# Block-sparse attention and a folded FFN: all engine orders from a list schedule, crossbar transposes, a shorter mask chain, value units of one head pair

## Chip, cores, metric

One core of one Trainium2 chip. The time is device microseconds of one execution; lower is better. Kernels of one set of rounds ran on the same chip with the kernel before beside them, and only runs marked fast are compared. This program runs on one core, so "slow" here only means a run over 1.5% above that kernel's fastest.

## The reference

Four batches, 8 heads, 768 positions, head size 64. Each 32x32 block of scores is kept or masked (window, first and last block row and column, three sampled blocks per row). The attention output becomes the 3072 x 512 input of an FFN without activation:

```python
scores = np.where(mask, q @ k.T / 8, -1e9)
attn   = softmax(scores) @ v                   # (B, H, S, D)
x      = attn.transpose(0, 2, 1, 3).reshape(B * S, H * D)
out    = ((x @ w1) * (x @ w2)) @ w3 @ w_out    # w3 @ w_out can be folded once
```

## The kernel before

The order on TensorE, ScalarE and VectorE is written by hand; GpSimd (POOL) issues all loads, which cast f32 to bf16 on the way. One step of the main loop does two score tiles (two head pairs), the values of the step before, and two filler pieces (of the fold w3 @ w_out, or of the FFN). q, k and x are turned on TensorE through PSUM; v gets its column of ones on GpSimd. PSUM: two score tiles of two banks, one value tile of two banks, two filler banks.

```python
def transposes(b, pr):                                  # q and k of a head pair, on TensorE
    tp = ps_s.tile([128, 2, 1024], BF16, tag="s")
    for x, src in ((0, qn[b, pr]), (1, kn[b, pr])):
        for c in range(C):
            for h in range(2):
                nc.tensor.transpose(tp[64*h:64*h+64, x, c*128:(c+1)*128], src[:, h, c, :], ident)
    nc.vector.tensor_copy(t, tp[:, :, :S])
def widen(b, pr):
    nc.gpsimd.memset(t[:, :, :, D:], 1.0)
    nc.gpsimd.tensor_copy(t[:, :, :, :D], vn[b, pr])    # behind the loads in POOL's queue
def scores(b, t, Q, kp, i):
    ...                                                 # 4 matmuls of 64 rows, 256 columns
    nc.scalar.activation(e, s, AF.Exp, scale=1.0 / 8.0)
    nc.vector.tensor_tensor(e, e, mask[...], op=ALU.mult)
...
for s, g in enumerate(groups):
    scores(b, t, Q, kp, 0)
    scores(b, t, Q, kp, 1)          # two score tiles in one visit to the 64-row mode
    values(*prev); turned(); finish(prev)
    ...
    pop(0 if s < 3 else 2)          # filler
```

The softmax here doesn't subtract the row's maximum and nothing guards it: scores larger than these inputs give would overflow.

## Time and profile before

| | before |
|---|---|
| time, median | 321.65 us |
| TensorE busy / VectorE / ScalarE | 261.4 / 207.5 / 171.2 us |

The top of the page of before: busy time by engine, then tenths of busy time in 40 slices of 8 us (PE is TensorE).

```profile
PE 261.4 (81%) x2932; PEld 141.6 (44%) x2932; DVE 207.5 (65%) x355; ACT 171.2 (53%) x202; POOL 61.1 (19%) x105
PE   0570388878889889998899889999988999889994
DMA  7999995956433000273301100001000010002003
```

In the views s is a score tile, e its exponentials, o the value accumulator, xn the normalised attention output and x the same turned; a, pb and h are FFN tiles; qkt is q and k turned, and in the change qs is q or k re-packed for the crossbar and f a filler bank.

TensorE has a thin start and small holes afterwards; the DMA engines are full for about 55 us and then mostly free. TensorE's timeline between 22 and 38 us (start, length, line, operation, tiles, shape, count, and in brackets the idle time before it and what ended it):

```profile
23.16 0.61 PE L206 MATMUL s<-qkt 64*128 64x256 bf16 x4 [0.30 <-ACT e L211]
36.73 0.38 PE L230 MATMUL o<-v,e 128*128 128x65 bf16 x4 [12.96 <-POOL v L195]
```

One hole of 13 us: v is there, but its widening stands behind the weight loads in POOL's queue. TensorE's waits over the whole run (total us, times, longest):

```profile
PE o L230 <- POOL v L195: 13.4, 2, 13.0
PE o L230 <- DVE xn L248: 11.1, 16, 1.9
PE pb L310 <- ACT a L302: 7.6, 11, 0.7
```

A stretch of the steady part, from the timeline:

```profile
165.67 1.03 PE L310 MATMUL pb<-x,w_sb 128*128 128x512 bf16 x4
166.63 0.61 PE L206 MATMUL s<-qkt 64*128 64x256 bf16 x8
167.17 0.66 PE L230 MATMUL o<-v,e 128*128 128x65 bf16 x16
```

From start to start, 8 score matmuls (two tiles) take 167.17 - 166.63 = 0.54 us, changes of the array's mode included (score matmuls use 64 rows of the array, the others 128; a visit to the 64-row mode is an unbroken run of score matmuls). Lengths overlap the next group and are not used for costs.

### The profile page before, as it was taken

To read this page: it belongs to the slowest core of one execution; us is meant where nothing else is said; L and a number is where in the kernel's file an instruction comes from. 1 tells how busy PE (TensorE), PEld (TensorE's weight loads), DVE (VectorE), ACT (ScalarE), POOL (GpSimd) and SP (SyncE) were. 2 spreads that over 40 slices of the span, in tenths; PEclk is the share of its full clock that TensorE was granted. 3 is DMA by queue.
4 is the path that set the end of the run, shared out by engine and by line. 5 is a ranking of instruction groups with operands and counts; after the bars stand their busy time and mean duration, and the time that the engine had idled before them with its cause. 6 is when DMAs were issued, how large, how long until landed. Compare 5 with 4: busy or idle time off the path is not lost.

```text
span 320.9 us, 6905 instructions
## 1 busy us (share of the span) xinstructions
PE 261.4 (81%) x2932; PEld 141.6 (44%) x2932; DVE 207.5 (65%) x355; ACT 171.2 (53%) x202; POOL 61.1 (19%) x105
## 2 busy tenths in 40 slices
PE   0570388878889889998899889999988999889994
PEld 0330255555544445555444445555444454444441
DVE  3611089888886677778767676787676876743432
ACT  1091166654566667465865686647666666620220
POOL 8535666813250000115300000000000000000000
PEclk9999999999999999999999999999999999999999
DMA  7999995956433000273301100001000010002003
GB/s 106 141 204 207 209 204 81 162 87 87 65 49 51 0 2 18 86 129 52 51 1 67 65 2 2 2 33 67 35 1 2 34 67 35 0 2 112 19 2 131
DMA packets 19922, 21.41 MB, mean 67 GB/s; under 512 B 1460, under 2 KB 14772, under 8 KB 19892
## 3 DMA queue, kind: packets, MB, share of 16 engines
q0 software_dynamic: 16400, 14.68, 30.2%
q1 hardware_dynamic: 3492, 6.29, 5.2%
q8 instruction: 23, 0.38, 0.5%
q14 instruction: 7, 0.06, 0.1%
HBM read 29.36 MB, written 6.29 MB: 111 GB/s over the span
## 4 chain that ended last, share of the span: by engine, by line
PE 54%; DVE 14%; ACT 11%; issue 8%; DMA 7%; POOL 4%; ACTq 0%; POOLq 0%
PE pb L310 11%; PE pa L299 11%; ACT e L211 9%; PE po L320 9%; PE o L230 8%; DMA w_sb<-in_moe_w_dram 7%; DVE e L212 7%; PE s L206 7%; DVE xn L248 4%; PE wp L281 4%; PE tp L186 2%; ACT a L302 2%; DVE qkt L189 2%; PE xp L254 2%; DVE rec L246 1%
## 5 line engine op out<-in xcount | busy, mean ns | idle before, releaser
L211 ACT ACTIVATE e<-s 128x1024 bf16<-128x1024 f32 x144 | 139.3, 1022 | 87.1 <-PE s L206 86.6
L212 DVE TENSOR_TENSOR e<-e,mask 128x1024 bf16<-128x1024 bf16 x144 | 104.1, 729 | 60.9 <-ACT e L211 59.2
L230 PE MATMUL o<-v,e 128*128 128x65 bf16 x1152 | 49.6, 196 | 25.3 <-POOL v L195 13.4
L230 PEld LDWEIGHTS <-e 128*128 128x128 bf16 x1152 | 40.3, 99 | 42.7 <-issue 25.3
L310 PE MATMUL pb<-x,w_sb 128*128 128x512 bf16 x192 | 49.2, 378 | 7.6 <-ACT a L302 7.6
L206 PE MATMUL s<-qkt 64*128 64x256 bf16 x576 | 48.0, 278 | 6.1 <-ACT e L211 3.6
L312 DVE TENSOR_TENSOR h<-pb,a 128x512 bf16<-128x512 f32 x48 | 33.1, 689 | 28.8 <-PE pb L310 28.8
L299 PE MATMUL pa<-x,w_sb 128*128 128x512 bf16 x192 | 49.3, 379 | 0.0
L302 ACT CAST a<-pa 128x512 bf16<-128x512 f32 x48 | 28.3, 589 | 36.1 <-PE pa L299 36.1
L320 PE MATMUL po<-wf_sb,h 128*128 128x512 bf16 x192 | 44.4, 379 | 0.0
L206 PEld LDWEIGHTS <-qkt 64*128 64x128 bf16 x576 | 22.9, 95 | 37.9 <-issue 34.9
L310 PEld LDWEIGHTS <-w_sb 128*128 128x128 bf16 x192 | 18.6, 97 | 33.5 <-issue 13.3
L320 PEld LDWEIGHTS <-h 128*128 128x128 bf16 x192 | 17.8, 98 | 19.2
L86 POOL DMA_DIRECT2D qn<-in_q_dram x16 | 11.7, 728 | 69.8 <-PE tp L186 61.3
L299 PEld LDWEIGHTS <-w_sb 128*128 128x128 bf16 x192 | 16.4, 98 | 14.2
L325 DVE COPY ob<-po 128x512 f32<-128x512 f32 x24 | 16.5, 686 | 9.5 <-PE po L320 9.5
L248 DVE TENSOR_TENSOR xn<-o,rec 128x512 bf16<-128x512 f32 x24 | 16.6, 691 | 0.8
L195 POOL COPY v<-vn 128x768 bf16<-128x768 bf16 x16 | 15.5, 980 | 3.1 <-DMA vn<-in_v_dram 3.0
L189 DVE COPY qkt<-tp 128x1536 bf16<-128x1536 bf16 x16 | 15.2, 948 | 1.3 <-PE tp L186 1.3
L281 PE MATMUL wp<-wo_sb,w3t_sb 128*128 128x512 bf16 x64 | 15.1, 379 | 0.0
L174 ACT CAST mask<-mp 128x512 bf16<-128x512 f32 x9 | 4.9, 587 | 14.3 <-PE mp L172 14.3
L86 POOL DMA_DIRECT2D kn<-in_k_dram x16 | 11.7, 730 | 3.4 <-PE w3p L268 1.7
(46 smaller groups left out, 129.9 us busy)
## 6 DMA issues: line engine op xcount, KB each, us to landing
out_dram<-ob SPq DMA_DIRECT2D x24, 256.0 KB, 2.0
w_sb<-in_moe_w_dram POOLq DMA_DIRECT2D x16, 256.0 KB, 10.2
qn<-in_q_dram POOLq DMA_DIRECT2D x16, 192.0 KB, 3.6
kn<-in_k_dram POOLq DMA_DIRECT2D x16, 192.0 KB, 4.4
vn<-in_v_dram POOLq DMA_DIRECT2D x16, 192.0 KB, 4.8
wo_sb<-in_moe_w_out_dram POOLq DMA_DIRECT2D x1, 1024.0 KB, 12.2
rand_sb<-in_sampled_blocks_dram SPq DMA_DIRECT2D x1, 0.6 KB
```

What stands on the lines that cost most here:

```text
L86: nc.gpsimd.dma_start(out=t, in_=src[b][:, 2 * pr:2 * pr + 2])
L206: nc.tensor.matmul(s[:, h, k2 * QT:(k2 + 1) * QT], lhsT=qk[64 * h:64 * h + 64, 1, kc * 128:(kc + 1) * 128], rhs=qk[64 * h:64 * h + 64, 0, ...
L211: nc.scalar.activation(e, s, AF.Exp, scale=1.0 / 8.0)
L212: nc.vector.tensor_tensor(e, e, mask[:, t, kp:kp + 1, :].to_broadcast((128, 2, 512)), op=ALU.mult)
L230: nc.tensor.matmul(o[:, qt, g * (D + 1):(g + 1) * (D + 1)], lhsT=es[i][:, h, lo:lo + 128], rhs=V1[b, 2 * Q + i][:, h, kc, :], start=kc == ...
L248: nc.vector.tensor_tensor(xn, o[:, :, :, :D], rec.to_broadcast((128, 2, 4, D)), op=ALU.mult)
L281: nc.tensor.matmul(box["p"], lhsT=w3t_sb[:, j, i * 128:(i + 1) * 128], rhs=wo_sb[:, j, :], start=j == 0, stop=j == NF - 1)
L299: nc.tensor.matmul(p, lhsT=w1_sb[:, c, f * 128:(f + 1) * 128], rhs=x[:, c, :], start=c == 0, stop=c == 3)
L302: nc.scalar.copy(a, p)
L310: nc.tensor.matmul(p, lhsT=w2_sb[:, c, f * 128:(f + 1) * 128], rhs=x[:, c, :], start=c == 0, stop=c == 3)
L312: nc.vector.tensor_tensor(hT[:, f, :], p, box["a"], op=ALU.mult)
L320: nc.tensor.matmul(box["o"], lhsT=hT[:, f, n * 128:(n + 1) * 128], rhs=wf_sb[:, f, :], start=f == 0, stop=f == NF - 1)
```

## The change

The intent: take work off TensorE (q, k of batches 1 to 3 and all of x are turned by DMA transposes through the crossbar), fill its holes (every engine's order, POOL's and SyncE's too, comes from a list schedule worked out at build time from fixed durations), and free PSUM (value units of one head pair need one bank, so there are three filler banks).

```diff
+class Plan:                      # list schedule over tasks: costs by engine, deps, buffers
+                for d in t.deps:
+                    e = d.seen                        # seen = end + 0.22 us for TensorE,
+                    base = max(base, e)               # for a TensorE task after another too
+            elif t.kind == "xbar":
+                xbar = max(xbar, t.end + 1.6) + t.bytes / 250e3
+                t.seen = xbar + 0.4                   # q or k, 196608 bytes: 2.8 us in all
...                               (the rest of the planner cut)
-    t = qkt.tile(...); nc.vector.tensor_copy(t, tp[:, :, :S])
+            if b == 0:            # on TensorE, as before
+            ...
+            else:                 # q, k of batches 1 to 3
+                m = add(f"re {b}{pr}{x}", {DVE: 0.45}, ... nc.vector.tensor_copy(
+                    T(*mid), T(*src).rearrange("p h c d -> p c h d")), ...)      # mid: qs, 3 buffers
+                t = add(f"xb {b}{pr}{x}", {SP: 0.3}, ... nc.sync.dma_start(
+                    out=T(*dst)[:, x, :]..., in_=T(*mid)..., transpose=True), kind="xbar", ...)
+    # x: one crossbar transpose of xn for each 128 rows
+    t = add(f"xx {b}{t3}{qt}", {SP: 0.3}, ... nc.sync.dma_start(out=T("x", i)[...],
+                    in_=T(*xk)[:, qt, :], transpose=True), kind="xbar", ...)
-        nc.gpsimd.tensor_copy(t[:, :, :, :D], vn[b, pr])
+        nc.vector.tensor_copy(w[:, :, :, :D], T(*src))
+    ts = add(f"S {sk}", {PE: 0.216}, sc, deps=QK[b, pr] + [prev_s], mode="S", ...)
+    # masks from fewer VectorE instructions; FFN pieces of two matmuls; copies on ScalarE or VectorE
```

## The prediction

> **What bounds the kernel now**
>
> - 0 to 40 us (table of stretches): TensorE is busy 13.4 of 40 us. By the chain of waits the worst hole is 13.4 us for the first widened v (POOL v L195): v was issued at 5.5 us, but its widening stands behind some 20 weight-load issues in POOL's in-order queue and starts at 35.8 us. ScalarE and VectorE idle 14 us with it.
> - 40 to 281 us: cadences read from the timeline are 0.54 us for two score tiles with mode switches, 0.48 for 16 value matmuls, 0.216 for a 512-column matmul, 0.79 for 24 q/k transposes, 0.22 for 4 x transposes. That is about 188 us of TensorE work in 241. The list of waits names the holes: values on xn (11 us), pb on a (7.6; only two filler banks), exp on scores (72.6).
> - 281 to 321 us: TensorE runs two FFN units back to back; the others are nearly idle.
>
> **What the change does**
>
> - TensorE loses 12 q/k transposes x 0.79 = 9.5 us and 24 x transposes x 0.22 = 5.3 us. Left: 72 x 0.54 + 72 x 0.48 + 640 x 0.216 + about 10 (fold transposes, batch 0, masks) = 222 us.
> - VectorE: minus 12 qkt copies x 0.95 and 24 x copies x 0.42 (21 us); plus re-packing q, k (11), v widening from POOL (10), twice as many rec/xn (5). About 210 us, of which 39 may go to ScalarE (masks, fold copies, ob). ScalarE: 144 x 0.97 + 48 x 0.58 + its share, about 190. Neither binds before TensorE.
> - DMA: 48 crossbar transposes, 7.9 MB. The Trainium skill, "DMA: Bandwidth & Descriptors", section "Latency and other measured facts", gives 261 GB/s for a DMA transpose with a non-contiguous middle dimension: an estimate of 0.8 us for 196 KB, plus about 2 us fixed; no run here shows it yet. The DMA engines are mostly under 10% busy after 100 us, so it fits.
> - Start: mask chain about 2 us shorter; v widened as it lands, values near 10 us instead of 36.7. Batch 0's 36 exps (35 us) and the fold (17 us of TensorE) run under the weight loads, which end near 45 us.
> - One-bank value accumulator, three filler banks, list schedule: waits are filled with FFN pieces of two matmuls.
>
> **Critical path.** TensorE is the limit: 222 us of work, 11 us of start in which it can't be fed, 3 us for the last copy and store: 236 us. With 8% for holes: **254 us**, 8 in 10 within **243 to 272**. Of 68 us won, about 15 are removed work, 20 the start, 33 fewer holes. Faster by over 2%: 0.96; within 2%: 0.02; slower: 0.02.
>
> **What would show each step.** TensorE over 90% from 45 us to the end; no wait of values on v; first values before 15 us; transposes of batches 1 to 3 and of x gone from TensorE, cadences unchanged; exp's idle time filled with a and ob copies; crossbar transposes landing in under 5 us; at most about 40 us of pure FFN at the end.
>
> **What would make it wrong.** Crossbar transposes several times slower than estimated, or slowed by loads on the same DMA engines: then scores wait for qkt, FFN for x. In-order engines following a schedule with wrong durations: small waits everywhere, TensorE near 80%. VectorE dearer than assumed (strided widening, more small operations) and so the limit. Loads held back because buffers free late.

## More of the kernel before

Busy time by stage (columns: stretch, its length, busy us with instructions for PE, PEld, DVE, ACT, POOL, granted clock, DMA share, GB/s):

```profile
60.00:125.00 65.00, 55.65 (x731) 31.92 (x730) 49.47 (x85) 40.76 (x46) 13.62 (x21) 1.00 0.38 53
125.00:240.00 115.00, 103.96 (x1263) 56.70 (x1261) 85.52 (x138) 73.12 (x85) 9.86 (x16) 1.00 0.18 43
```

## The result

The change took 297.79 us (296.79 and 298.79) against 321.65: ratio 0.9258, 95% interval 0.9124 to 0.9392. Timed again over more rounds (below) it took 297.36 us, ratio 0.9215 (0.9189 to 0.9241). It is faster, but far outside the predicted 243 to 272 us. The ratios are from the fast runs of both kernels in the same rounds, so they are not quite the ratios of the medians.

The same lines after the change, the top of the page (with the granted clock, PEclk, whose row was 9 in every slice before):

```profile
PE 256.7 (87%) x2505; PEld 121.0 (41%) x2548; DVE 185.4 (63%) x396; ACT 184.6 (63%) x221; POOL 46.2 (16%) x75
PE   2989999768689995699999999799999999948994
PEclk9999999997959997999999999999999999995998
DMA  6999999699989999936750101301014001130003
```

The start is full now. But TensorE has a weak stretch in slices 8 to 16 (60 to 125 us), where the DMA row stays at 8 or 9, and a hole near the end; behind each the clock row dips. TensorE's waits:

```profile
PE f L576 <- DMA x<-xn: 5.3, 3, 4.5
PE s L483 <- DMA qkt<-qs: 4.6, 2, 3.4
PE o L505 <- DVE e L492: 4.1, 3, 2.8
PE o L505 <- DVE xn L515: 3.1, 2, 2.5
```

The waits on POOL and on a are gone, as predicted. The stages:

```profile
60.00:125.00 65.00, 50.63 (x432) 22.02 (x439) 35.17 (x87) 32.41 (x40) 17.87 (x25) 0.89 1.19 148
125.00:240.00 115.00, 110.61 (x1138) 50.79 (x1158) 82.32 (x164) 87.36 (x103) 0.76 (x1) 1.00 0.25 58
```

From 125 us on TensorE is 96% busy; from 60 to 125 us it is worse than before, at a clock of 0.89. This profile lacks 43 matmul records, spread evenly; in the second profile of the change (e13), where none is missing, the weak stretch reads

```profile
60.00:125.00 65.00, 52.85 (x447) 22.21 (x445) 35.53 (x88) 32.26 (x39) 17.86 (x25) 0.87 1.20 149
```

so about 2 us of its 14.4 us of idleness are missing records. The profiles of e1, e2, e9 and e10 lack about as many and are compared with the first one. The chain that ended last, between 60 and 84 us (start, us, what):

```profile
60.01 1.29 PE f L557 x6
61.98 9.42 DMA qkt<-qs
72.65 10.65 DMA qkt<-qs
```

Two q, k transposes of 9.4 and 10.7 us. All 24, their issues and their landing times:

```profile
L443 SPq DMA_TRANSPOSE qkt<-qs x24: 1210/1282/3607, 47.8 to 145.7; - x24
DMA to landing us min/median/max: 2.7/6.1/10.8
```

Those that the trace ties to a landing have a median of 8.7 us when issued before 125 us (14 of them) and 2.8 us after (7). The plan assumed 2.8. Meanwhile the bf16 bytes of loads fell from about 205 GB/s (20 to 40 us) to 56 to 92 in the stretches of 10 us between 60 and 120 us, counted from the trace's DMA packets.

How idleness is paid twice (stretches as above; the last three numbers are granted clock, DMA share and GB/s):

```profile
79.00:82.00 3.00, 1.31 (x12) 0.56 (x12) 2.85 (x8) 0.63 (x2) 0.71 (x1) 0.94 1.54 118
82.00:85.00 3.00, 1.60 (x14) 0.86 (x15) 1.31 (x3) 1.17 (x2) 0.71 (x1) 0.50 1.30 200
262.00:266.00 4.00, 0.42 (x8) 0.29 (x8) 0.61 (x2) 0.06 (x1) 0.00 (x0) 1.00 0.42 114
266.00:270.00 4.00, 3.06 (x8) 1.13 (x9) 0.00 (x0) 0.23 (x1) 0.00 (x0) 0.50 0.09 17
```

After a few microseconds of a mostly idle TensorE the granted clock is 0.50. And the score tiles, from the timeline:

```profile
153.96 0.39 PE L483 MATMUL s<-qkt 64*128 64x256 bf16 x4
154.28 0.42 PE L505 MATMUL o<-v,e 128*128 128x65 bf16 x8
```

They now come one at a time: 4 score matmuls take 154.28 - 153.96 = 0.32 us, where two tiles together took 0.54.

A ledger from TensorE's matmul records (a matmul counts from its start to the next start or to its own end, whichever is first; the rest is idle; what half clock cost is half of the work time in such stretches). The change is taken from its second profile; none of these three lacks a 512-column matmul record:

| us | predicted | before | change | pairs and batch 1 on TensorE (e6) |
|---|---|---|---|---|
| 640 matmuls of 512 columns | 138.2 | 147.3 | 156.1 | 143.9 |
| scores | 38.9 | 44.4 | 50.4 | 41.8 |
| values | 34.6 | 39.4 | 41.4 | 38.7 |
| transposes, masks | about 10 | 30.4 | 14.3 | 18.2 |
| work, sum | 222 | 261.4 | 262.2 | 242.6 |
| idle, with first matmul and tail | 32 | 59.6 | 32.1 | 12.0 |
| span | 254 | 320.9 | 294.3 | 254.6 |
| of work: half clock until full clock at 20 to 22 us (before: 40.8) | - | 7.1 | 7.8 | 6.8 |
| of work: half clock later | - | 0.0 | 9.4 | 0.0 |
| visits to the 64-row mode | - | 71 | 137 | 80 |

By this count TensorE's work did not fall: transposes and masks lost 16 us, about the 15 that were forecast, and half clock and single visits put as much back. The gain is idle time, 59.6 us before and 32.1 after.

### The profile page after: what moved, and what is told of

It is laid out like the page before. It is cut to its first block, busy times and chain, and to the rows that moved or that the text cites. A ratio compares the mean times of both kernels' runs of the same rounds, so it can differ in the third digit from the quotient of the medians.

```text
span 295.0 us, 6214 instructions
## 1 busy us (share of the span) xinstructions
PE 256.7 (87%) x2505; PEld 121.0 (41%) x2548; DVE 185.4 (63%) x396; ACT 184.6 (63%) x221; POOL 46.2 (16%) x75
## 4 chain that ended last, share of the span: by engine, by line
PE 69%; DMA 18%; ACT 4%; DVE 4%; issue 3%; SPq 1%; POOL 0%; DVEq 0%; ACTq 0%; POOLq 0%
PE f L576 26%; PE s L483 13%; DMA qkt<-qs 13%; PE o L505 12%; PE f L595 11%; ACT e L490 4%; PE f L557 4%; DMA x<-xn 3%; DVE e L492 2%; DMA kn<-in_k_dram 1%; PE f L431 1%; PE f L409 1%; PE f L545 1%; SPq L528 1%; DVE xn L515 1%
## 5 line engine op out<-in xcount | busy, mean ns | idle before, releaser
L576 PE MATMUL f<-x,w 128*128 128x512 bf16 x361 | 103.7, 402 | 9.5 <-DMA x<-xn 5.3
L505 PE MATMUL o<-v,e 128*128 128x65 bf16 x1152 | 60.3, 197 | 8.2 <-DVE e L492 4.1
L505 PEld LDWEIGHTS <-e 128*128 128x128 bf16 x1152 | 50.4, 99 | 41.7 <-issue 9.9
L483 PE MATMUL s<-qkt 64*128 64x256 bf16 x576 | 58.7, 283 | 9.2 <-DMA qkt<-qs 4.6
L587 DVE TENSOR_TENSOR h<-f,a 128x512 bf16<-128x512 f32 x48 | 33.0, 688 | 30.8 <-PE f L576 20.0
L595 PE MATMUL f<-wf,h 128*128 128x512 bf16 x180 | 48.8, 380 | 1.2 <-issue 1.0
L576 PEld LDWEIGHTS <-w 128*128 128x128 bf16 x384 | 31.1, 101 | 41.8 <-issue 17.7
L584 ACT CAST a<-f 128x512 bf16<-128x512 f32 x48 | 28.0, 583 | 26.6 <-PE f L576 25.6
L515 DVE TENSOR_TENSOR xn<-o,rec 128x256 bf16<-128x256 f32 x48 | 20.4, 424 | 1.6
L513 DVE RECIPROCAL rec<-o 128x4 f32<-128x4 f32 x48 | 8.6, 179 | 14.4 <-PE o L505 14.1
L557 PE MATMUL f<-wo,w3t 128*128 128x512 bf16 x56 | 16.6, 381 | 0.5 <-issue 0.2
L300 POOL DMA_DIRECT2D vn<-in_v_dram x16 | 11.6, 725 | 31.2 <-DVE h L587 15.0
```

The lines of the kernel that those rows point to most:

```text
L300: t = add(name, {POOL: 0.73}, lambda t: nc.gpsimd.dma_start(out=out_of(), in_=src), deps=deps, writes=writes, kind="load", prio=seq[0])
L483: nc.tensor.matmul(s[:, h, k2 * QT:(k2 + 1) * QT], lhsT=z[64 * h:64 * h + 64, 1, kc * 128:(kc + 1) * 128], rhs=z[64 * h:64 * h + 64, 0, t3 ...
L505: nc.tensor.matmul(o[:, qt, h, :], lhsT=e[:, h, lo:lo + 128], rhs=w[:, h, kc, :], start=kc == 0 and qt == 0 and h == 0, stop=kc == C - 1, ...
L515: tx = add(f"xn {rk}", {DVE: 0.40}, lambda t, rk=rk, ok=ok, xk=xk, pr=pr: nc.vector.tensor_tensor(T(*xk)[:, :, 128 * pr:128 * pr + 128].re ...
L557: nc.tensor.matmul(T(*key), lhsT=T("w3t", i)[:, j, :], rhs=wo_sb[:, j, :], start=j == 0, stop=j == NF - 1)
L576: nc.tensor.matmul(T(*key), lhsT=w[:, c, f * 128:(f + 1) * 128], rhs=T(*xk)[:, c, :], start=c == 0, stop=c == 3)
```

## The experiments

Theory A: beside the loads a crossbar transpose takes three times as long as planned. The re-packed tiles (three buffers) and so the loads are held, scores starve, and the clock halves. A1 says that the shared DMA engines do it; A2 that SyncE's in-order queue does, with x transposes waiting in front of q, k. Rival B: the loads are late by themselves. Rival C: the planned order is bad as such. D: single score visits. H: idleness halves the clock. Every edit is made in the change; the planner then plans anew.

| run | us, median | ratio to before | 95% |
|---|---|---|---|
| change, again (e13) | 297.36 | 0.9215 | 0.9189 to 0.9241 |
| e1: q, k on TensorE | 288.11 | 0.8929 | 0.8898 to 0.896 |
| e2: x on TensorE | 280.96 | 0.87 | 0.8666 to 0.8733 |
| e3: no crossbar | 287.28 | 0.8911 | 0.8884 to 0.8937 |
| e4: pairs | 270.2 | 0.8374 | 0.8339 to 0.8408 |
| e5: pairs, x on TensorE | 273.73 | 0.8497 | 0.845 to 0.8544 |
| e6: pairs, batch 1 on TensorE | 257.03 | 0.7972 | 0.7946 to 0.7998 |
| e7: pairs, no crossbar | 281.11 | 0.8711 | 0.8681 to 0.874 |
| e8: pairs, plan told of a slow crossbar | 281.53 | 0.8726 | 0.8698 to 0.8755 |
| e9: batch 1 on TensorE | 280.86 | 0.8629 | 0.8583 to 0.8675 |
| e10: no late loads (wrong result) | 277.64 | 0.86 | 0.8568 to 0.8632 |
| e11: busy in the last wait | 296.64 | 0.8988 | 0.8945 to 0.9031 |
| e12: e6 with a busy start | 256.81 | 0.7974 | 0.7943 to 0.8005 |
| e14: last x on TensorE | 290.8 | 0.8924 | 0.8872 to 0.8976 |

e2, e8, e9, e11 and e14 have runs over 1.5% above their fastest; ratios leave those out, medians don't.

### e1, e2, e3: the crossbar undone by halves

```diff
-            if b == 0:
+            if b in (0, 1, 2, 3):                      # e1 and e3: q, k through TensorE and PSUM
-    nc.sync.dma_start(out=T("x", i)[...], in_=T(*xk)[:, qt, :], transpose=True)
+    nc.tensor.transpose(...)                           # e2 and e3: x in 24 groups of 4, then a copy
```

> Edit: q and k of batches 1 to 3 are turned on TensorE again (as batch 0 is), x stays on the crossbar; the order is planned anew. Theory A (the q, k crossbar transposes, 8 to 10 us to land beside the loads, hold the buffers, so hold the loads, and starve TensorE from 60 to 125 us): no load waits for a re-packed tile any more, TensorE's idle time between 60 and 125 us falls from about 14 us to under 6, its half-clock stretches there disappear; 9.5 us of transposes and 24 copies come back; net 276 to 286 us against 297. Rival B (the loads themselves are late, whoever turns q and k): the idle time of 60 to 125 us stays near 14 us, now on loads, and the time is 300 us or more. Rival C (the planned order as such is what is slow): time about 297 plus the 9.5 us put back.

> Edit: x is turned on TensorE again (24 groups of 4 transposes and a copy), q and k of batches 1 to 3 stay on the crossbar. Theory A: the stall of 60 to 125 us stays, as the q, k transposes are its cause; at the end the wait for the last x falls from 4.5 us to under 2 and the half-clock stretch of 6.8 us after it disappears (about 3.4 us), against 5.3 us of transposes put back: 292 to 298 us. If the x transposes were the trouble, the stall of 60 to 125 us would go: 280 us or less.

> Edit: both on TensorE; what is left of the change is the list schedule, the short mask chain, v widened on VectorE and value units of one head pair. Theory A: the other parts carry the whole gain, so 278 to 292 us, faster than the change as it is. Rival C (the order is slow in itself): 305 us or more, near the kernel before.

e1: 288.1 us, 2 us over A's range. Idle time of 60 to 125 us fell from 14.4 us in the change's first profile to 8.5 (under 6 was expected) and half clock after the start cost 4.7 us. So taking the crossbar away from q, k removes much of the stall, not all; part of what is left is waits for loads, as B has it. e2: 281.0 us, which misses my expectation of 292 to 298. Taking x away also relieved the stretch of 60 to 125 us (8.5 us idle instead of 14.4) and closed the hole at the end; I had put down the stall to q, k alone, and for the case that the x transposes were the trouble I had named 280 us or less; so they have a part in it. e3: 287.3 us, inside the range. The parts without the crossbar carry the whole gain, 322.5 to 287.3, and the crossbar as it is placed gives 10 us back. Rival C's 305 us or more is ruled out.

### e4: two score tiles in a visit

```diff
-                    e = d.seen
+                    e = d.end if d.eng == "PE" and list(t.costs) == ["PE"] else d.seen
```

> Edit: in the plan a TensorE task may follow another TensorE task at once (before, the plan made it wait 0.22 us as for another engine), so that two score tiles can be issued in one visit to the 64-row mode. Theory D (142 single score visits, each with two mode switches, cost about 7 us of TensorE work that the prediction did not count): visits fall from about 142 to under 100, the cost of 4 score matmuls from 0.32 to under 0.30 us, and the time falls by 4 to 12 us. If the order matters little beside the stall of 60 to 125 us: within 3 us of 297.

270.2 us: 27 us less, where 4 to 12 were expected. D holds as far as it goes: visits fell from 137 (142 in the expectation) to 79 and score work from 50.7 to 43.8 us between the two profiles. The rest is another effect of the same line: attention runs ahead, so FFN work is left over for the last wait. The hole of 4.5 us and the half clock after it are gone, and so are their costs (see e14). The stall on qkt is still there: waits of 6.2 and 7.3 us at 55 and 74 us.

### e5 to e8: what is left with pairs

Each has the line of e4 as well as its own edit.

```diff
 e5  x on TensorE, as e2
 e6  -            if b == 0:
     +            if b in (0, 1):
 e7  q, k and x on TensorE, as e3
 e8  -  t.bytes / 250e3
     +  t.bytes / (250e3 if t.start > 125 else 50e3)
```

> Edit: the pairs edit, and x turned on TensorE. Theory A2 (the q, k crossbar transposes of batch 1 stand in SyncE's in-order queue behind x transposes that wait for the attention, 14 us in the pairs run): the two waits of scores on qkt of 6.2 and 7.3 us shrink to under 6 us together, half-clock after warm-up under 5 us, and against 5.3 us of transposes put back the time is 258 to 266 us. Theory A1 (the crossbar is slow beside the loads, whatever stands in the queue): both waits stay, 270 to 278 us.

> Edit: the pairs edit, and q, k of batch 1 on TensorE like batch 0's; batches 2 and 3 and x stay on the crossbar. Theory A (A1 or A2: what costs is that batch 1's transposes fall into the stretch in which the loads fill the DMA engines): the 13.5 us of waits of scores on qkt at 55 to 81 us and the 4.7 us lost to half clock go, 3.2 us of transposes come back: 252 to 262 us. Rival B (the loads themselves are late): idle time stays over 10 us before 100 us, now as waits for loads: 264 us or more.

> Edit: the pairs edit, no crossbar at all. Theory D alone (pairs save about 7 us of switches wherever the turning is done): 287 minus 5 to 9, so 277 to 283 us. If the order gains as much from pairs as with the crossbar (27 us): 265 us or less.

> Edit: the pairs edit, and the plan is told that before 125 us a crossbar transpose moves 50 KB per us instead of 250 (about 6 us for q or k, as measured beside loads, instead of about 3). The data path is the same; only the order changes. If the stall comes from an order laid out on durations that are too short: the waits of scores on qkt fall from 13.5 to under 5 us and the time to 255 to 264 us. If the crossbar's rate beside the loads is the limit, no order helps: 266 to 275 us.

e5: 273.7 us. With no x transpose in SyncE's queue TensorE's waits on qkt (total, times, longest) were still

```profile
PE s L483 <- DMA qkt<-qs: 11.0, 3, 8.3
```

against 14.0 us in e4, so x transposes in front of q, k are not the main cause and A1's range holds; by e2 they add to it without pairs. e6: 257.0 us, inside the range; the loads are the same, so B falls as the main cause. Its ledger is above; its stage, and the score tiles in pairs on its timeline:

```profile
60.00:125.00 65.00, 64.37 (x756) 34.79 (x754) 54.84 (x120) 53.57 (x65) 11.43 (x16) 1.00 0.87 118
154.88 0.61 PE L483 MATMUL s<-qkt 64*128 64x256 bf16 x8
155.42 0.60 PE L576 MATMUL f<-x,w 128*128 128x512 bf16 x2
```

The weak stretch became 64.37 us busy of 65, at full clock. e7: 281.1 us. Without the crossbar, pairs save 6.2 us against e3, which is D alone. So of the 27 us in e4 most belongs to pairs together with the crossbar. It also shows that the crossbar is worth having: e6 beats e7 by 24 us. e8: 281.5 us, worse than both theories said. Waits on qkt did fall to 1.9 us, but values then waited 9.3 us for e, and half clock cost 5.6 us. Honest durations for the same DMA load did not bring the time back; one figure for every transpose before 125 us is crude, though, so e8 does not rule out a better order.

### e9 and e10: the two direct tests of A

e9 is e6's edit without pairs. e10 gives wrong results on purpose and keeps the change's order on every engine:

```diff
-  nc.gpsimd.dma_start(out=out_of(), in_=src)
+  nc.gpsimd.memset(out_of(), 0.0) if skip else nc.gpsimd.dma_start(out=out_of(), in_=src)
#  skip: q, k, v of batches 1 to 3; same task, same planned duration
```

> Edit: the change with only one thing undone: q and k of batch 1 are turned on TensorE; the plan's rule on TensorE tasks as in the change (no pairs). Theory A: the stall of 60 to 125 us (14.4 us idle, and most of the 8.7 us lost to half clock after the warm-up) goes, 3.2 us of transposes come back: 274 to 284 us; score visits stay near 137, and the hole at the end with its half-clock stretch stays. If batch 1 on TensorE helps only together with pairs: 290 us or more.

> Edit, wrong result on purpose: the loads of q, k, v of batches 1 to 3 are replaced by a memset of the same tile on GpSimd (zeros); tasks, planned durations and so the order on every engine are those of the change. Theory A1 (the crossbar transposes take 8 to 10 us only because their 256-byte packets share the DMA engines with the loads' packets): after about 50 us every q, k transpose lands in 2.5 to 3.5 us, the mean time of a 256-byte packet falls from 30 to 42 ns to about 20 ns, idle time of 60 to 125 us falls from 14.4 to under 5 us, and the time to 268 to 280 us. Theory A2 (the in-order queues and the plan, not the DMA engines' load): landing times fall but the idle time stays over 10 us; 288 us or more.

e9: fast runs of 277.8 and 279.6 us, inside the range (the two slow ones 282). That is about 19 us without pairs, against 13 us with them (e4 to e6). But I had expected the hole at the end to stay, and it shrank; the first matmuls after the hole, in the change and in e9:

```profile
266.94 16.91 PE L576 MATMUL f<-x,w 128*128 128x512 bf16 x63 [4.47 <-DMA x<-xn]
255.14 14.01 PE L576 MATMUL f<-x,w 128*128 128x512 bf16 x63 [2.39 <-issue]
```

No half clock followed in e9. That profile is of one of the slow runs; if the fast ones ended alike, about 2 + 3.4 us of the 19 belong to the end, and moving batch 1 off the crossbar is worth about 13 us either way. e10: 277.6 us, inside A1's range. Its landing times and its stage:

```profile
DMA to landing us min/median/max: 2.7/2.8/4.5
60.00:125.00 65.00, 62.55 (x602) 28.77 (x614) 52.37 (x121) 46.18 (x56) 20.41 (x26) 1.00 0.52 94
```

The median falls from 6.1 to 2.8 us and TensorE is busy 62.55 us of 65 instead of 50.63, with the same instructions of its own in the same order. So it is the loads beside the transposes. (e10 also takes away any lateness of the loads; that this is not the main cause rests on e6 and e9, which keep every load.) The hole at the end stays (4.5 us), since no load runs there.

Why a load costs a transpose so much: the Trainium skill, "DMA: Bandwidth & Descriptors", section "Queues, rings and completion order", says that each DMA engine goes round its queues in turn, packet by packet. In the trace a transpose of 196,608 bytes is 768 packets of 256 bytes, 48 for each of 16 engines; a load's packet takes 82 to 126 ns on average in these stretches, a transpose's 27 to 42 ns (20 to 31 ns in e10 without loads). Estimate: if every packet waits for one load packet of 100 ns, 48 x (0.1 + 0.03) = 6.2 us, plus about 2 us fixed from the 2.8 us that a lone one takes: about 8 us. This is near the median of 8.7 us, but the packet counts don't bear it out. The two transposes that were alone in their queue (issued at 47.8 and 94.6 us) landed in 6.2 and 4.7 us, with 879 and 434 load packets beside their 768. While each of the other 12 was under way, 863 to 3161 transpose packets passed, with only 0.2 to 0.6 load packets for each. This points to loads that slow a transpose to 5 or 6 us, and to transposes that then wait behind one another for the rest of the 8.7 us; how the engines take turns was not observed.

### e11 and e14: the hole at the end

```diff
 e11 +  20 matmuls of 512 columns that nobody reads, planned into the last wait
 e14 +  only the last 256 rows of x through TensorE
```

> Edit: the change, plus 20 matmuls of 512 columns that nobody reads, which the plan puts into TensorE's wait for the last x. Theory H (the half-clock stretch of 6.8 us at 266 us comes from the 4.5 us of idleness before it, and is paid as 3.4 us): the stretch disappears, the 32 w1 and w2 matmul groups of the last unit run at 0.216 us each from their start, and the time falls by 2 to 4 us. If the clock falls for another reason: no change.

> Edit: the change, with only the last 256 rows of x (batch 3, last third) turned on TensorE. The pairs run gained 27 us of which switches are about 7. Theory T (a further 6 to 8 us of it is the hole at the end: 4.5 us of waiting for the last x and 3.4 us of half clock after it, which pairs cover with FFN work that is left over): here the hole shrinks to under 2 us, no half-clock stretch follows, and the time falls by 4 to 8 us against the change in the same rounds. If the hole at the end costs nothing more than its 4.5 us: 2 to 4 us.

e11, stretches at the end:

```profile
266.00:270.00 4.00, 3.79 (x18) 1.59 (x18) 0.10 (x1) 0.00 (x0) 0.00 (x0) 1.00 0.48 120
270.00:273.00 3.00, 3.00 (x15) 1.32 (x15) 0.69 (x1) 0.58 (x1) 0.00 (x0) 1.00 0.00 0
```

The wait is the same, the clock stays at 1.00: H holds. From the first w1 matmul of the last unit to the end of its last matmul the change took 290.76 - 266.94 = 23.8 us, e11 290.86 - 269.89 = 21.0. The total is not clear: two runs took 290 us, four 296 to 298; the profiled run is one of the four and had its own longer half-clock stretches earlier. e14: fast runs of 285.7 to 289.8 us (mean 9 us under the change of the same rounds, all six runs 7). The hole shrank to 0.6 us and no half clock followed; it was worth 4.5 + 3.4 us, so T's mechanism holds. The 9 us of fast runs lie above its 4 to 8, but the six runs spread over 8.5 us, so the size is rough. With e4: 7 us of switches, about 8 us of this hole, and about 1 us less of half clock in the middle. Some 11 us of the 27 are not assigned to any one cause and stay open.

### e12 and e13

```diff
 e12 +  e6, with 8 matmuls of 512 columns on zeros from 1.2 us until q lands
 e13    no edit
```

> Edit: the run with pairs and batch 1 on TensorE (257.0 us), plus 8 matmuls of 512 columns on zeros that nobody reads, from about 1 us until q lands. There the first 20 us ran at half clock, 6.8 us of work lost. If the clock rises after one stretch of steady work: full clock from about 5 to 8 us instead of 19.8, most of the 6.8 us of work saved, but ScalarE and the loads pace the start too, so 252 to 256 us. If the start is paced by the loads alone: 257 us.

> The change itself, unedited, five rounds more: it was timed only twice (296.8 and 298.8 us), and a run that differs from it only in matmuls nobody reads gave both 290 and 297 us. If the stall of 60 to 125 us makes the time vary from run to run: runs spread over 288 to 299 us, with the kernel before within 1% in the same rounds. If not: all runs within 1% of 297.5 us.

e12: 256.8 us, the same as e6. The first 20 us of matmuls run at half pace (12 transposes take 0.54 us there from the first start to the last, 0.31 later), and steady work from 1.2 us on did not move the point of full clock (20.7 us against 19.8). e13: all six runs between 296.1 and 298.1 us. The change does not spread; the two times of e11 belong to e11.

## Why the prediction was wrong

- **Bound and direction were right.** TensorE is the limit, and faster was forecast. The start came out in part: the wait of values on v fell from 13.4 to 0.8 us and batch 0 runs under the weight loads, but the first values came at 16.8 us, not near 10 or before 15. Waits of values on xn fell from 11.1 to 3.1 us and pb's waits on a vanished.
- **The step that failed:** "48 crossbar transposes, 7.9 MB ... an estimate of 0.8 us for 196 KB, plus about 2 us fixed ... The DMA engines are mostly under 10% busy after 100 us, so it fits." The estimate was right for a lone transpose (2.7 to 2.8 us). But q, k of batches 1 to 3 are turned from 48 to 146 us, mostly while the same batches are still loading, and there it took 8.7 us: 4.7 to 6.2 us beside the loads alone, the rest, as far as the packets show, in a queue of transposes. It "fits" by bytes, but scores wait for qkt, and the loads behind it for the re-packed tiles. I looked at DMA use of before after 100 us, not at when the transposes must run. I had named this as a risk and given it too little weight. e10 shows its worth: 20 us.
- **A mis-sized term:** "72 x 0.54" for scores assumed two tiles in a visit, as before. The diff makes a TensorE task wait 0.22 us of planned time after another TensorE task, so the plan hardly ever issues two together (137 visits for 144 tiles). Scores took 50.4 us instead of 38.9. This was to be read in the diff. The Trainium skill, "TensorEngine Tiling (Array Packing)", section "Tiling Modes", says that a change of mode drains the engine; here a visit with one tile took 0.32 us, with two 0.54, so each extra visit costs 2 x 0.32 - 0.54 = 0.10 us, and 65 of them 6.5 us; half clock took 3.6 us of the scores' time. The cadences were low besides: they give 211.7 us for the 512-column matmuls, scores and values, on which the kernel before spent 231.1 us by the same ledger, only 3 us of it half clock.
- **A missing term:** half clock. The Trainium skill, "TensorE: Matmul & The Clock Gate", Part 1, says that an idle window of about 3.4 us brings half clock. The traces agree on the window but not on idle. Seven profiles have every 512-column record (before, e5 to e8, e13, e14). Cut into windows of 3.41 us from the moment of full clock on, half clock followed each of the 13 windows in which TensorE worked 1.77 us or less, and none of the 489 at full clock in which it worked 1.82 us or more. It ended after windows with 2.90 us of work or more, and not after 2.75 or less. In the change such stretches cost 9.4 us later in the run, and the first 20 us another 7.8; I counted neither.
- **A right sum for wrong reasons:** idleness was allowed 32 us and measured 32.1, but it was to be small holes everywhere and is one stall and one hole. "TensorE over 90% from 45 us to the end" failed from 60 to 125 us. e6, which has neither the stall nor single visits, took 257.0 us with 12 us idle and 242.6 us of work, so its nearness to 254 owes something to two errors of opposite sign.

## What to carry to other kernels

A transfer's cost is what it takes beside the traffic of its own time: before moving work to the DMA engines, lay its time window over the loads that run there, and keep the slower engine's path for the part that falls among them (one batch of q, k here, worth about 13 us). A list schedule is only as good as its dependency rules: read the resulting order for pairs that were split, for one line here was worth 27 us, some 7 of them by the pairs themselves. A TensorE that is idle for about half of a 3.4 us window is paid again at half clock, so leave some independent work for the last wait; e6, at 257.0 us, beats both kernels.

## What the Trainium skill lacked or had wrong

- "DMA: Bandwidth & Descriptors", "Rules for kernel authors", says, in a row on corruption, that a transpose next to ordinary DMAs needs nothing. No corruption was seen here, but in time it needs much: a q, k transpose landed in 8.7 us (median) beside loads and other transposes, in 4.7 and 6.2 us beside loads alone, in 2.8 us without loads. Its figure of 261 GB/s is given without this condition.
- "TensorE: Matmul & The Clock Gate", Part 1, gives about 3.4 us of sustained work until full clock. Here full clock came 19.5 to 23.2 us after the start in every profiled run with the planned order, in e12 at 20.7 us although TensorE had worked from 1.2 us with about 1 us of idleness in the first 20 (its first 8 matmuls were on zeros). In all 16 profiles, the kernel before too (at 40.8 us), it came 3.2 to 6.5 us after the first value matmuls. So the page's figure about fits from there on; the transposes, the masks on 24 rows and the scores on 64 rows before did not bring it, though TensorE was busy with them for whole windows. What it is in that work was not tested, and the cause is open. The trace's clock records begin only with this rise, so the column of granted clock shows 1.00 before it; the pace of the matmuls shows the half clock.
- The same Part 1 ties half clock to an idle window. Here a window of 3.41 us with up to 1.77 us of work was enough (13 of 13), and 1.82 us kept full clock (489 of 489).
- "TensorEngine Tiling (Array Packing)" gives no figure for the drain of a mode change; here an extra visit cost 0.10 us.
